# Moving two head pairs of the next batch's scores into the slot of the low-rank down-projection

## Chip, cores and metric

The kernel runs on one core of one Trainium2 chip. The metric is the device time of one launch in microseconds (us). Three runs of the kernel before gave 316.07, 316.18 and 316.94 us, median 316.18 us.

## What is computed

Sliding-window causal attention (window 64) over 8 batches, 8 heads, 576 tokens and head size 64, then a mixer: a low-rank mixing over the tokens, and a two-layer MLP over the 512 channels, each with a residual.

```python
scores = scale * np.matmul(q, k.transpose(0, 1, 3, 2))
mask = (rel >= 0) & (rel < window)          # window = 64
attn = softmax(np.where(mask, scores, -1e9))
x = np.matmul(attn, v)                      # -> (8, 576, 512), heads side by side

h = x.transpose(0, 2, 1) @ U @ V            # over tokens, rank 32
u = x + h.transpose(0, 2, 1)
out = u + np.maximum(u @ w_ch1, 0.0) @ w_ch2   # 512 -> 2048 -> 512
```

## The kernel before

**Two streams in one program.** The MLP works on 4608 tokens as nine chunks `c` of 512 tokens. Each chunk has 32 slots. Slots 0 to 15 are the up-projection: `ch1(i)` issues four matmuls of 128x512 into a PSUM tile `psA` (L671) and a ReLU that writes `c1[i]`, on VectorE for the `i` in `DVE_RELU`/`DVE_RELU_N` and on ScalarE for the others. Slots 16 to 31 are the down-projection: `ch2(t, quarter)` issues four matmuls into `psU` (L694), and each fourth one ends with the residual add on VectorE (`osb`, L703) and a store that SyncE issues (L706). So slots 19, 23, 27 and 31 end with a store.

**The next batch rides along.** While chunk `c` runs, the pieces of batch `b = c + 1` are put behind single slots: a table `PLACE` (with `PLACE_1`, `PLACE_2`, `PLACE_3` for the first batches) gives for each kind of piece the slot after which it is issued. There is no scheduler: each engine's instructions stand in the order in which this loop issues them, and an engine waits at an instruction until its semaphores are there.

```python
for fill, extra in zip(mlp(c) + [lambda: None], slots):
    fill()
    for f in extra:
        f()
```

The kinds of pieces are:

- **T**, from batch 2 on: `TX(t)`, two DMA transposes (L311) that SyncE issues, one for the keys (`kf<-kr`) and one for the queries (`qf<-qr`) of the 128 tokens of tile `t`, t = 0 to 4. They stand in the chunk that `CROSS` names, otherwise in slots 20 to 24 of chunk `b - 3`. They write one of two buffers, by the batch's parity. SyncE's queue also holds the stores of the output and the UT transposes, all in one order.
- **S**: first `SC8` (the last block of queries for all heads, tiles `low` and `high`), then `SC(j)` for the four head pairs j = 0 to 3: 36 matmuls of 64x64 or 64x128 into `sc` for two pairs (L352), and an exponential on ScalarE into `pts[:, j]` (L372). An `SC(j)` reads the transposed tiles t = 0 to 3 of its batch in this order; block pairs that cross into tile 3 need its queries.
- **M**: the 0/1 mask on VectorE, one for `SC8` (L385) and one for each head pair (L378).
- **PV**: `PVA`, the products with the values into four PSUM tiles, then the division on VectorE into `xs` (L470 to L493).
- **U**: `UM`, the low-rank down-projection from `xs` into `pshh` (L513, L521) and a copy to `hh` on ScalarE (L528).
- **V**: `VM`, the up-projection of the rank into `psv` (L593) and the addition on VectorE into `un` (L606), for tiles (0, 1), (2, 3) and (4).
- **UT**: a DMA transpose of `un` into the MLP's operand `uTc` (L621), from batch 3 on; SyncE issues it. Chunk 3 needs tiles 0, 1 and 2 of batch 3.

Before the change the entries for the steady batches were these, so that all five scores of a batch stood in slots 0 and 3 of its own chunk:

```python
"S": [0, 0, 0, 3, 3],
"M": [0, 1, 2, 4, 5],
"PV": [8],
"U": [14],
"V": [16, 17, 18],
"UT": [17, 17, 18, 18, 19],
```

**PSUM.** `ps_big` (two tiles of two banks, tag `big`) serves `sc`, `xw`, `pshh` and `psv` in turn; `ps_tp` (one bank) serves `low`, `one` (the last values of a batch) and the transposes of the first batches; `psum["mm"]` has three banks for `psA`, `psU`, `high` and `xe`.

**Loads.** GpSimd's queue loads K, Q and V of later batches and casts them (L128, L137, L142).

Of the kernel before, what the change touches and what calls it, by code (L numbers as in the profile page):

```python
# [12 lines left out]
FP32 = mybir.dt.float32  # L13
# [3 lines left out]
def kernel(  # L17
# [12 lines left out]
    B, H, S, D = q.shape  # L30
# [3 lines left out]
    P = nc.NUM_PARTITIONS  # L34
# [12 lines left out]
    CH = 512  # L47
# [17 lines left out]
    ps_big = ctx.enter_context(tc.tile_pool(name="ps_big", bufs=2, space=bass.MemoryType.PSUM))  # L65
    ps_tp = ctx.enter_context(tc.tile_pool(name="ps_tp", bufs=1, space=bass.MemoryType.PSUM))
# [81 lines left out]
    def shift_v(b, copy, tiles):  # L148
        va, vb = vA[b % 2], vB[b % 2]
        lo, hi = tiles.start, tiles.stop  # L150
        copy(out=vb[W:P, lo:hi, :, :], in_=va[W:P, lo:hi, :, :])
        last = min(hi, NFULL - 1)
        if lo < last:
            copy(out=vb[0:W, lo:last, :, :], in_=va[0:W, lo + 1 : last + 1, :, :])

    def shift_high(b, copy, t):
        copy(out=vB[b % 2][W:P, t, :, :], in_=vA[b % 2][W:P, t, :, :])  # L157
# [103 lines left out]
    def attention(b, spare=False):  # L261
# [6 lines left out]
        pcs = {}  # L268
# [106 lines left out]
        def MK(j):  # L375
            def f():
                dst = pts[:, j, :, :, :].rearrange("p g n w -> p g (n w)")
                nc.vector.tensor_tensor(  # L378
                    out=dst, in0=dst, in1=maskA.rearrange("p g n w -> p g (n w)"), op=ALU.mult
                )  # L380
            return f
# [25 lines left out]
        def values(dst, h, blk):  # L407
            if blk == 0:
                rhs = va[:, 0, h, :]
            elif blk % 2 == 1:  # L410
                rhs = va[:, blk // 2, h, :]
            else:
                rhs = vb[:, blk // 2 - 1, h, :]
            nc.tensor.matmul(  # L414
                dst,
                pts[:, h // 2, h % 2, blk, :] if blk < NB - 1 else ptl[:, h // 2, h % 2, :],
                rhs,
                start=True,
                stop=True,
            )  # L420

        def PV(t):
            def f():
                blks = [bl for bl in (2 * t - odd, 2 * t + 1 - odd) if 0 <= bl < NB]
                lo = W if (odd and t == 0) else 0
                hi = W if (not odd and t == NT - 1) else P

                xr = ps_big.tile([P, 2, CH], FP32, name="xr", tag="big")
                for h in range(H):
                    for blk in blks:  # L430
                        r0 = ((blk + odd) % 2) * W
                        cols = slice((h % 4) * VW, (h % 4 + 1) * VW)
                        values(xr[r0 : r0 + W, h // 4, cols], h, blk)
                xv = xr[lo:hi, :, 0 : 4 * VW].rearrange("p a (h e) -> p a h e", e=VW)
                rcp = wk_pool.tile([P, 2, 4, 1], FP32, name="rcp", tag="rcp")
                nc.vector.reciprocal(out=rcp[lo:hi], in_=xv[:, :, :, D:VW])
                nc.vector.tensor_tensor(
                    out=x[lo:hi, t, :, :].rearrange("p (a h) d -> p a h d", a=2),
                    in0=xv[:, :, :, 0:D],
                    in1=rcp[lo:hi].to_broadcast([hi - lo, 2, 4, D]),  # L440
                    op=ALU.mult,
                )
            return f
# [56 lines left out]
        hh = {}  # L500
        xc = lambda src, t, dc: src[:, t, :, :].rearrange("p h d -> p (h d)")[:, dc * P : (dc + 1) * P]

        def UM(ts):
            def f():
                if ts[0] == 0:
                    if spare:
                        hh["ps"] = psum["spare"].tile([P, CH], FP32, name="psh", tag="spare")
                    else:
                        hh["ps"] = ps_big.tile([P, 2, CH], FP32, name="pshh", tag="big")[:, 0, :]
                for t in ts:  # L510
                    xt = x[:, t, :, :].rearrange("p h d -> p (h d)")
                    if t < 4:
                        nc.tensor.matmul(  # L513
                            hh["ps"][t * R : (t + 1) * R, :], ub[odd][:, t, :], xt,
                            start=True, stop=False,
                        )
                        continue

                    for g in range(4):
                        cols = slice(g * P, (g + 1) * P)  # L520
                        nc.tensor.matmul(  # L521
                            hh["ps"][g * R : (g + 1) * R, cols], ub[odd][:, t, :], xt[:, cols],
                            start=False, stop=True,
                        )
                if ts[-1] == NT - 1:
                    hh["sb"] = wk_pool.tile([P, CH], BF16, name="hh", tag="hh")
                    for cs in (slice(0, CH // 2), slice(CH // 2, CH)) if spare else (slice(0, CH),):
                        nc.scalar.copy(out=hh["sb"][:, cs], in_=hh["ps"][:, cs])  # L528
            return f
# [108 lines left out]
        if not spare:  # L638
            pcs["M"] = [MK(j) for j in range(HP)]
            pcs["M"].insert(0 if b >= NGR else HP, MK8)  # L640
        pcs["PV"] = [PVA] if not spare else [PV(t) for t in range(NT)]
        pcs["U"] = [UM((t,)) for t in range(NT)] if spare else [UM(tuple(range(NT)))]
        if spare:
# [12 lines left out]
        return pcs  # L656


    DVE_RELU = {0: (7, 9, 11, 15), 1: (4, 7, 9, 10, 11, 13, 14), 2: (2, 3, 4, 6, 7, 8, 10)}
    DVE_RELU_N = (0, 1, 2, 4, 5, 6, 8)  # L660

    def mlp(c):
        uTc = uT_of(c)
# [2 lines left out]
        def ch1(*ids):  # L666
            def f():
# [10 lines left out]
                for i in ids:  # L678
                    c1[i] = c1_pool.tile([P, CH], BF16, name=f"c1_{i}")
                    if i in DVE_RELU.get(c, DVE_RELU_N):  # L680
                        nc.vector.tensor_relu(out=c1[i][:], in_=ps[i][:])  # L681
# [32 lines left out]


    PLACE = {
        "S": [0, 0, 0, 3, 3],
        "M": [0, 1, 2, 4, 5],
        "PV": [8],
        "U": [14],  # L720
        "V": [16, 17, 18],
        "UT": [17, 17, 18, 18, 19],
    }
    PLACE_0 = {"V": [0, 0, 1, 2, 2, 3, 4, 4]}
    PLACE_1 = {
# [21 lines left out]
        "SV": [7, 7, 8, 8],  # L747
        "PV": [10],
        "U": [16],
        "V": [18, 19, 20],  # L750
        "UT": [18, 18, 19, 19, 20],
    }
    CROSS = {
        0: {2: [16, 17, 18, 19, 20]},
# [82 lines left out]
    for c in range(NCH):  # L837
        slots = all_slots[c]

        def place(b, parts, where):  # L840
            if b not in att:
                att[b] = attention(b)
            for part in parts:
                for f, s in zip(att[b][part], where[part]):
                    all_slots[c + s // 100][s % 100].append(f)

        b = c + 1
        if b < B:
            if b == 1:
                for _ in load_kq(2, False):  # L850
                    pass

            def load_next(b=b):
                for _ in load_kq(b + 2, False):
                    pass

            if 1 < b and b + 1 < B:
                load_v(b + 1)
            if 1 < b and b + 2 < B:
                load_next()  # L860
            where = {1: PLACE_1, 2: PLACE_2, 3: PLACE_3}.get(b, PLACE)
            if b < NXB:
                place(b, ("T",), where)
            if b == 1:
                place(0, ("V",), PLACE_0)
                slots[6].append(lambda: nc.scalar.copy(out=ub[1][:], in_=uf[1][:]))
            if 3 < b + 1 < B:
                slots[24].append(
                    lambda bs=b + 1: shift_v(bs, nc.vector.tensor_copy, range(NFULL))
                )  # L870
            if b <= 3:

                def land(t, b=b):
                    def f():
                        shift_high(b, nc.scalar.copy, t)
                        if t > 0:
                            shift_low(b, nc.vector.tensor_copy, t - 1)
                    return f

                att[b]["SV"] = [land(t) for t in range(NFULL)]  # L880
                place(b, ("SV",), where)
            place(b, ("S", "M", "PV"), where)
            for n, at in CROSS.get(c, {c + 3: CROSS_N}).items():
                if n < B:
                    place(n, ("T",), {"T": at})
            place(b, ("U", "V", "UT"), where)
            if b == 1:

                def after(t):
                    return lambda: nc.gpsimd.tensor_copy(  # L890
                        out=held[:], in_=qfs[0][0:1, t * HP * P : t * HP * P + 1]
                    )

                slots[20] += [after(2), lambda: load_v(2), after(NT - 1), load_next]
# [4 lines that stand above are left out]
# [30 lines left out]
```

## Time and profile before

| | before |
|---|---|
| time, median of 3 runs | 316.18 us |
| profiled execution, its own time | 316.14 us |
| its span, first to last instruction | 314.4 us |
| TensorE matmul busy | 306.2 us, 97% of the span |
| VectorE / ScalarE / GpSimd busy | 162.4 / 110.8 / 98.8 us |
| first `psA` matmul of chunk 2 / 3 / 4 | 94.06 / 126.73 / 158.81 us |
| last load issued on GpSimd's queue | 184.0 us |

The profile is one execution. "PE" is TensorE's matmuls, "PEld" its weight loads, DVE VectorE, ACT ScalarE, POOL GpSimd, and SPq the issue of DMAs on SyncE. The chain is the work that ended last, followed back from the end. A timeline row gives start and duration in us, engine, line, operation and tiles (output, then inputs), and a count where rows are merged; in square brackets is the engine's idle time before it, and what ended it. A DMA's row on SPq is the time of its issue; the time to its landing is longer and is told apart.

### The profile page before, as it was taken

Reading aid. Unit: us, or ns where it says so; the run is one execution under the profiler, and the core shown is the slowest. Engines: PE = TensorE matmul, PEld = TensorE weight load, DVE = VectorE, ACT = ScalarE, POOL = GpSimd, SP = SyncE. Lnnn points to the kernel's source line nnn. Section 1 sums busy time; section 2 is a strip of 40 time slices with the busy share of each in tenths; the row PEclk is TensorE's granted clock in tenths of the full one; section 3 lists DMA queues with packets and bytes.
Section 4 is the critical chain, followed back from the end, with each engine's and each line's share of the span. In section 5 each row is a group of like instructions: output and inputs, shape, how many; then the busy total and the mean of one; then the engine's idle time right before and its main releaser. Section 6 shows DMA issues by size and latency. Waiting matters only on the chain.

```text
span 314.4 us, 6910 instructions
## 1 busy us (share of the span) xinstructions
PE 306.2 (97%) x2875; PEld 149.3 (47%) x2875; DVE 162.4 (52%) x297; ACT 110.8 (35%) x178; POOL 98.8 (31%) x129
## 2 busy tenths in 40 slices
PE   8889999999999999999999999999999999999994
PEld 7444554544454544454445444544454444444441
DVE  4465477428645944684358445844574343016011
ACT  3575590358127620633053304440344003201500
POOL 8584154279555445343553440000000000000000
PEclk9999999999999999999999999999999999999999
DMA  7999999999999999999999999924100510011011
GB/s 112 162 187 207 196 163 139 153 196 172 137 151 188 157 166 183 174 143 152 158 174 145 174 152 156 163 68 118 69 2 2 149 68 2 33 67 35 0 67 67
DMA packets 152255, 39.34 MB, mean 125 GB/s; under 512 B 140928, under 2 KB 147072, under 8 KB 152224
## 3 DMA queue, kind: packets, MB, share of 16 engines
q0 software_dynamic: 100624, 18.36, 77.9%
q1 hardware_dynamic: 51600, 20.55, 38.3%
q8 instruction: 22, 0.36, 0.5%
q14 instruction: 9, 0.07, 0.1%
HBM read 36.92 MB, written 9.44 MB: 147 GB/s over the span
## 4 chain that ended last, share of the span: by engine, by line
PE 91%; DMA 4%; DVE 3%; ACT 1%; issue 0%; POOLq 0%
PE psA L671 40%; PE psU L694 36%; PE psv L593 3%; PE sc L352 3%; DMA uTc<-un 2%; PE xw L414 2%; DMA kr<-in_k_dram 2%; PE tpg L288 1%; DVE xs L481 1%; PE sc L342 1%; PE tpu L625 1%; PE pshh L513 1%; ACT pts L372 1%; PE tpm L288 1%; PE xr L414 1%
## 5 line engine op out<-in xcount | busy, mean ns | idle before, releaser
L671 PE MATMUL psA<-uTc,w1b 128*128 128x512 bf16 x576 | 130.8, 379 | 0.7 <-DVE uTc L580 0.4
L694 PE MATMUL psU<-w2b,c 128*128 128x512 bf16 x576 | 131.2, 379 | 0.1
L694 PEld LDWEIGHTS <-c 128*128 128x128 bf16 x576 | 55.5, 98 | 65.7 <-issue 0.8
L671 PEld LDWEIGHTS <-w1b 128*128 128x128 bf16 x576 | 54.1, 98 | 65.3 <-issue 2.7
L683 ACT ACTIVATE c<-psA 128x512 bf16<-128x512 f32 x84 | 50.1, 597 | 89.5 <-PE psA L671 88.5
L703 DVE TENSOR_TENSOR osb<-psU,un 128x512 f32<-128x512 f32 x36 | 24.7, 691 | 75.5 <-PE psU L694 75.2
L681 DVE TENSOR_SCALAR c<-psA 128x512 bf16<-128x512 f32 x60 | 41.4, 690 | 27.5 <-PE psA L671 27.5
L606 DVE TENSOR_TENSOR un<-psv,xs 128x512 bf16<-128x512 f32 (+1 forms) x40 | 25.6, 685 | 22.9 <-PE psv L593 22.7
L128 POOL DMA_DIRECT2D kr<-in_k_dram x30 | 25.4, 848 | 24.2 <-DMA vA<-in_v_dram 14.3
L137 POOL DMA_DIRECT2D vA<-in_v_dram x32 | 28.3, 893 | 15.1 <-DMA kr<-in_k_dram 4.0
L372 ACT ACTIVATE pts<-sc 128x1024 bf16<-128x1024 f32 x32 | 31.3, 1030 | 3.9 <-PE sc L352 3.9
L128 POOL DMA_DIRECT2D qr<-in_q_dram x30 | 25.4, 846 | 21.5 <-DMA vA<-in_v_dram 13.6
L405 ACT ACTIVATE ptl<-low 128x256 bf16<-128x256 f32 x6 | 2.3, 384 | 62.0 <-PE high L352 62.0
L378 DVE TENSOR_TENSOR pts<-pts,maskA 128x1024 bf16<-128x1024 bf16 x28 | 19.1, 682 | 0.1
L481 DVE TENSOR_TENSOR xs<-xw,rcw 128x896 bf16<-128x896 f32 x14 | 15.3, 1092 | 0.5
L352 PEld LDWEIGHTS <-kf 64*64 64x64 bf16 x704 | 9.7, 107 | 7.3 <-issue 7.1
L593 PE MATMUL psv<-hh,vrep 128*128 128x512 bf16 x40 | 12.6, 379 | 0.0
L352 PE MATMUL sc<-qf,kf 64*64 64x128 bf16 (+1 forms) x608 | 11.5, 212 | 0.7 <-DVE qf L305 0.5
L414 PEld LDWEIGHTS <-pts 128*64 128x64 bf16 x512 | 9.9, 110 | 4.3 <-issue 3.0
L628 ACT COPY uTc<-tpu 128x512 bf16<-128x512 bf16 x9 | 5.3, 585 | 10.8 <-PE tpu L625 10.8
L157 ACT COPY vB<-vA 64x520 bf16<-64x520 bf16 x15 | 8.4, 618 | 0.4 <-DMA vA<-in_v_dram 0.3
L414 PE MATMUL xw<-vA,pts 128*64 128x65 bf16 x217 | 8.5, 195 | 0.0
(108 smaller groups left out, 162.8 us busy)
## 6 DMA issues: line engine op xcount, KB each, us to landing
out_dram<-osb SPq DMA_DIRECT2D x36, 256.0 KB, 3.9
vA<-in_v_dram POOLq DMA_DIRECT2D x32, 128.0 KB, 13.4
kr<-in_k_dram POOLq DMA_DIRECT2D x24, 128.0 KB, 11.9
qr<-in_q_dram POOLq DMA_DIRECT2D x24, 128.0 KB, 11.7
w2b<-in_moe_w_ch_dram POOLq DMA_DIRECT2D x4, 512.0 KB, 15.3
w1b<-in_moe_w_ch_dram POOLq DMA_DIRECT2D x2, 512.0 KB, 11.1
w1b<-in_moe_w_ch_dram POOLq DMA_DIRECT2D x1, 1024.0 KB, 9.1
kr<-in_k_dram POOLq DMA_DIRECT2D x2, 288.0 KB, 5.4
```

The costliest lines, as they stand in the source:

```text
L128: nc.gpsimd.dma_start(out=dst[0:rows, t, :, :], in_=src[b, :, t * P : t * P + rows, :].rearrange("h p d -> p h d"),)
L137: nc.gpsimd.dma_start(out=va[:, t, :, 0:D], in_=v[b, :, t * P : (t + 1) * P, :].rearrange("h p d -> p h d"),)
L352: nc.tensor.matmul(sc[g][r0 : r0 + W, col * W : (col + n) * W], keys_of(j, u, rs), queries_of(j, blk, n, rs), start=not spare, stop=last o ...
L372: nc.scalar.activation(out=dst, in_=sc[:], func=ACT.Exp, scale=scale)
L414: nc.tensor.matmul(dst, pts[:, h // 2, h % 2, blk, :] if blk < NB - 1 else ptl[:, h // 2, h % 2, :], rhs, start=True, stop=True,)
L593: nc.tensor.matmul(ps[0][:, n, :], vrep[:, off : off + P], hh["sb"][:], start=True, stop=True)
L606: nc.vector.tensor_tensor(out=u_tiles[g][rs, :], in0=ps[0][rs, n, :], in1=x[rs, t, :, :].rearrange("p h d -> p (h d)"), op=ALU.add,)
L671: nc.tensor.matmul(ps[i][:], w1b[:, dc, i * P : (i + 1) * P], uTc[:, :, dc, :], start=(dc == 0), stop=(dc == NDC - 1),)
L681: nc.vector.tensor_relu(out=c1[i][:], in_=ps[i][:])
L683: nc.scalar.activation(out=c1[i][:], in_=ps[i][:], func=ACT.Relu)
L694: nc.tensor.matmul(acc[t][:], c1[i][:, t * P : (t + 1) * P], w2b[:, i, :], start=(i == 0), stop=(i == NFC - 1),)
L703: nc.vector.tensor_tensor(out=osb[:], in0=acc[t][:], in1=u_tiles[g][:], op=ALU.add)
```

## The change

From batch 4 on (`AHEAD = 4`) the list S of a batch is cut: `SC8`, `SC(0)` and `SC(1)` stay in slot 0 of its own chunk, and `SC(2)` and `SC(3)` become "S+", with their masks as "M+". S+ and M+ of batch `b + 1` are placed while batch `b` is, in the chunk before their own: directly behind `UM` of batch `b`. For the steady batches that is slot 11, and PV, U and their masks move to it: PV from slot 8 to 5, U from 14 to 11, V and UT one slot sooner. In chunk 2, where batch 3 is prepared, U stays in slot 16, S+ of batch 4 goes behind it, and V and UT move one slot later. `pshh` is taken from `ps_tp` rather than from `ps_big`, for all batches but batch 0. The ReLUs that VectorE takes in steady chunks change from 0, 1, 2, 4, 5, 6, 8 to 0, 1, 2, 4, 11, 12, 13. The number of instructions does not change.

```diff
@@ UM @@
-                        hh["ps"] = ps_big.tile([P, 2, CH], FP32, name="pshh", tag="big")[:, 0, :]
+                        hh["ps"] = ps_tp.tile([P, CH], FP32, name="pshh", tag="tp")[:]
@@ attention, the lists of pieces @@
+        if b >= AHEAD:
+            for part in "SM":
+                pcs[part + "+"] = pcs[part][3:]
+                pcs[part] = pcs[part][:3]
@@
+    AHEAD = 4
+
-    DVE_RELU_N = (0, 1, 2, 4, 5, 6, 8)
+    DVE_RELU_N = (0, 1, 2, 4, 11, 12, 13)
@@ PLACE @@
-        "S": [0, 0, 0, 3, 3],
-        "M": [0, 1, 2, 4, 5],
-        "PV": [8],
-        "U": [14],
-        "V": [16, 17, 18],
-        "UT": [17, 17, 18, 18, 19],
+        "S": [0, 0, 0],
+        "M": [0, 1, 2],
+        "PV": [5],
+        "U": [11],
+        "S+": [11, 11],
+        "M+": [13, 14],
+        "V": [15, 16, 17],
+        "UT": [16, 16, 17, 17, 18],
@@ PLACE_3 @@
-        "V": [18, 19, 20],
-        "UT": [18, 18, 19, 19, 20],
+        "S+": [16, 16],
+        "M+": [17, 18],
+        "V": [19, 20, 21],
+        "UT": [19, 19, 20, 20, 21],
@@ the placing loop @@
-            place(b, ("U", "V", "UT"), where)
+            place(b, ("U",), where)
+            if AHEAD <= b + 1 < B:
+                place(b + 1, ("S+", "M+"), where)
+            place(b, ("V", "UT"), where)
```

## Prediction

> **What bounds the kernel now.** I read the page's busy times first, then the chain of work that ended last, then the timelines of TensorE and SyncE where the change acts.
>
> ```profile
> PE 306.2 (97%) x2875; PEld 149.3 (47%) x2875; DVE 162.4 (52%) x297; ACT 110.8 (35%) x178; POOL 98.8 (31%) x129
> PE 91%; DMA 4%; DVE 3%; ACT 1%; issue 0%; POOLq 0%
> ```
>
> TensorE bounds it, and its matmuls hardly wait: the chain runs through PE for 91%. A busy PE need not be at its peak, so I take starts. Where the MLP runs alone the chain has 64 `psA` in 13.81 us, 0.216 us each, 0.863 us a slot. Against that pace two waits are left in the middle of the kernel: 0.22 us at 52.84 us, and 0.38 us where chunk 3 begins, for `uTc`. The rest of the excess is about 0.09 us at each turn between 128x512 matmuls and the smaller ones: `psA` x12 at 128.38 takes until 131.08, 2.70 us for 12 x 0.216 = 2.59. So only turns can be saved, and any new wait on PE is added in full.
>
> TensorE around U of chunk 2 and chunk 3, where S+ will stand (timeline):
>
> ```profile
> 111.92 0.40 PE L513 MATMUL pshh<-xs,ub 128*32 128x512 bf16 x4
> 112.30 1.90 PE L694 MATMUL psU<-w2b,c 128*128 128x512 bf16 x8
> ...
> 126.73 1.02 PE L671 MATMUL psA<-uTc,w1b 128*128 128x512 bf16 x4 [0.22 <-DMA uTc<-un]
> 131.08 0.65 PE L352 MATMUL sc<-qf,kf 64*64 64x128 bf16 x36
> 131.66 1.69 PE L671 MATMUL psA<-uTc,w1b 128*128 128x512 bf16 x7
> ...
> 142.66 0.40 PE L513 MATMUL pshh<-xs,ub 128*32 128x512 bf16 x4
> ```
>
> The two pairs that move cost 131.66 - 131.08 = 0.58 us and a turn. What they read comes from SyncE's transposes. These are the issues for tile 3 of batch 4's keys and queries, and for the first and last that batch 5's moved scores need:
>
> ```profile
> 105.89 2.08 SPq L311 DMA_TRANSPOSE kf<-kr  x1
> 108.08 1.23 SPq L311 DMA_TRANSPOSE qf<-qr  x1
> ...
> 124.23 1.48 SPq L311 DMA_TRANSPOSE kf<-kr  x1
> 136.19 2.35 SPq L311 DMA_TRANSPOSE qf<-qr  x1
> ```
>
> The rows are issues only. The trace's answer on the tile `qf`, cut to the one at 108.08 and then to the one at 136.19, gives from issue to landing:
>
> ```profile
> DMA to landing us min/median/max: 7.9/7.9/7.9
> DMA to landing us min/median/max: 10.1/10.1/10.1
> ```
>
> So batch 4's queries of tile 3 are there at 108.08 + 7.9 = 116.0, batch 5's at 146.3. In the same way batch 6's (issued 163.59, 9.4 us) land at 173.0 and batch 7's (197.95, 4.5 us) at 202.5. Before, each is first read in its own chunk, 10 or more us later.
>
> [...] So a score that waits holds up all `psA` and `psU` behind it. [...] the last matmul starts at 310.5 and the granted clock is 0.50 from 313.8:
>
> ```profile
> 310.50:313.80 3.30, 0.01 (x1) 0.00 (x0) 0.69 (x1) 0.00 (x0) 0.00 (x0) 1.00 0.21 79
> 313.80:314.40 0.60, 0.00 (x0) 0.00 (x0) 0.00 (x0) 0.00 (x0) 0.00 (x0) 0.50 0.00 0
> ```
>
> The third column from the right is the clock. [...] `uTc` transposes land in 2.4 us at best, after the loads are done, but in 7.2 us at 119.39.
>
> **The change, part by part.**
>
> *Turns.* S in slot 3 had two turns and U two; U and S+ in one slot have three. Four batches (4 to 7) save one each: 4 x 0.09 = -0.4 us. Bounds: 0 (turning from U to S+ costs two), -0.75 (it costs none).
>
> *Chunk 2, S+ of batch 4.* U ends at 112.30 (unchanged up to there: PE and SyncE have the same order). S+ starts at 112.4, does the pairs within tiles 0 to 2 (the last landed at 112.7), and stands until 116.0 + 0.1. A third of the 0.58 us is done before, so 0.39 remains: end 116.5 instead of 113.0. **+3.5 us** (3.2 to 3.8). Behind it on PE is every `psU` of chunk 2, on ScalarE two exponentials (1.03 us each), on VectorE two masks, then the `un` additions that feed UT.
>
> *Chunk 3's start.* V is now in slot 19. After a turn and slots 17 to 19 (3 x 0.863) `psU` of that slot ends at 119.2; VectorE's `osb` (0.69) and two additions (0.68 each) end at 120.1, 120.8, 121.4. SyncE's order is now store, UT(0), UT(1), UT(2): 120.1 + 1.2 for the store as at 118.08, 1.3 each, so UT(2) is issued at 124.0 and lands with 7.2 us at 131.2. PE has finished chunk 2 at 116.5 + 15 x 0.863 + 5 x 0.216 + 0.1 = 130.6. It waits 0.6 to 0.7 us where it waited 0.38: **+0.3 us** (-0.4 if landing takes under 6.6 us, +1.2).
>
> *Chunk 3, S+ of batch 5.* SyncE goes on: UT(3), UT(4), the store of slot 23, and batch 5's first transpose at 128.6 instead of 124.23. From that to the landing of the eighth took 146.3 - 124.2 = 22.1 us here, 20.4 for batch 6, 19.5 for batch 3; [...] I take 21.3: landing 149.9 (bounds 148.1, 150.7). Chunk 3 starts at 131.3. U came 15.93 us after the start; without three slots and slot 3's scores it comes 15.93 - 2.59 - 0.68 = 12.66 after: 143.9, S+ at 144.4. It stands until 150.0; less the 0.2 us done before: **+5.4 us** (3.6 to 6.9, with SyncE a little late).
>
> *Chunk 4, S+ of batch 6.* Let S+ of chunk 3 end at E. UT(0) follows 4.8 us later, and as in chunk 3 before (146.14 to 152.60, to a landing at 173.0) batch 6 is in at E + 4.8 + 26.9 = E + 31.7. PE needs 18.6 us to chunk 4 and 13.2 to S+: E + 31.8. A tie: **+0.2 us** (0 to 1.5). Batch 7's transposes took 16.7 us, shorter by 3.7: no wait.
>
> *The clock.* The wait in chunk 2 is 3.2 us idle, just under what the end of the trace shows; that in chunk 3 about 5.4. [...] I take 0.6 x 2 = **+1.1 us** (0 to 2.9; more if chunk 2 is caught too).
>
> *At nothing.* Values three slots sooner: their loads are in (batch 5's last at 147.9, read after 165; batch 4's 117.5, read after 137). `pshh` in `ps_tp`: the tile before it there is `one`, emptied by the last of the divisions (L493), which U awaits anyway; were that cover gone it would cost 0.4 us a batch. Masks and ReLUs: from slot 11 to 19 VectorE has 3 ReLUs, 2 masks and 5 additions, 10 x 0.68 = 6.8 us, in some 9 us of PE (8 slots, U, S+, `psv`); ScalarE has the copy and two exponentials, 2.6 us, before its next ReLU 2.6 us later, and three `psA` banks between.
>
> *Sum:* 3.5 + 0.3 + 5.4 + 0.2 + 1.1 - 0.4 = 10.1. The profiled execution took 316.14 us in all, 0.04 below the median, so **326.2 us**.
>
> **Rivals.**
>
> 1. *Only turns change* (faster or same). If the transposes land before S+ reaches them, 315.4 to 316.2. It is decided at 112.4 and 144.4: tile 3 must have landed. SyncE issues in the same order up to 108.08, so chunk 2's landing can only move by noise. Against it: 3.6 us. Chance 0.03.
> 2. *Only the first wait.* PE's own delay gives SyncE time. It would need batch 5 in 5 us sooner, a landing of 5 us instead of 10, seen only once loads end. 316.2 + 3.5 + 0.3 - 0.4 = 319.6, with a rest up to 321.5. Chance 0.10.
> 3. *Half clock twice, and a wait in chunk 4.* 326.2 + 1.8 + 2 + 1.5 = 331.5 and more. Chance 0.10.
> 4. *VectorE becomes the bound* behind the masks: only if slots 11 to 19 hold over 9 us of its work; they hold 6.8. It would add under 0.5 us a chunk, and is in the range.
>
> **Numbers.** The main case has 0.77: 322 to 330.5. With some of 2 and 3 the range is 321.5 to 331. A measurement here tells about 0.3% (0.95 us) from no change. Faster by that 0.01 (even all turns saved give 0.75), same 0.02, slower 0.97.
>
> **What would show it.** In the profile after: `sc` L352 waiting for DMA `qf` in chunk 2 near 112.5 for 3 us and in chunk 3 near 144.5 for 5, a new share of DMA in the chain, PEclk below 9 in the slice after. No wait in chunk 5. I am wrong if the chain stays on PE throughout, if chunk 3 shows under 3 us, or if the delay sits on DVE or ACT.

## Result and profile after

The changed kernel is slower: 331.40 us median of 4 runs (327.89 to 333.51) beside 316.56 us for the kernel before, also 4 runs; the ratio is 1.043, with a 95% interval of 1.034 to 1.052. This ratio, like all below, leaves out executions more than 1.5% above the fastest of their kernel, here the one of 333.51, which the medians take in. The profiled execution of the changed kernel took 327.89 us, 11.75 us more than that of the kernel before, and its span is 326.2 us.

The page's busy times, clock and chain, as they were read before:

```profile
PE 309.5 (95%) x2875; PEld 150.9 (46%) x2875; DVE 163.5 (50%) x297; ACT 111.4 (34%) x178; POOL 98.9 (30%) x129
PEclk9799999999999999995999999999999999999999
PE 70%; DMA 15%; issue 5%; POOL 4%; DVE 3%; ACT 1%; POOLq 0%
```

No engine got more instructions. The chain has lost 21 points on PE and gained 11 on DMA, and one slice in the middle has half the clock. TensorE's timeline at the moved scores shows where; first chunk 2 (batch 4's pairs), then the start of chunk 3, then batch 5's pairs in chunk 3:

```profile
115.34 0.35 PE L352 MATMUL sc<-qf,kf 64*64 64x128 bf16 x12
116.28 0.50 PE L352 MATMUL sc<-qf,kf 64*64 64x128 bf16 x24 [0.58 <-DMA qf<-qr]
...
131.81 1.02 PE L677 MATMUL psA<-uTc,w1b 128*128 128x512 bf16 x4 [0.89 <-DMA uTc<-un]
...
144.85 0.30 PE L352 MATMUL sc<-qf,kf 64*64 64x128 bf16 x8
146.22 0.25 PE L352 MATMUL sc<-qf,kf 64*64 64x128 bf16 x4 [1.07 <-DMA qf<-qr]
150.85 0.80 PE L352 MATMUL sc<-qf,kf 64*64 64x128 bf16 x24 [4.38 <-DMA qf<-qr]
```

Of the 36 score matmuls 8 or 12 go at once; the other 24, among them those that read the queries of tile 3, stand in the bracket, and every `psA` and `psU` stands behind them. The bracket counts from the modelled end of the matmul before. Taken from start to start against TensorE's pace (0.216 us for 512 columns, 0.58 us for 36 scores), these waits are 0.75, 1.05, 1.23 and 4.57 us.

The time from one chunk's first `psA` to the next shows the sum:

| from the first `psA` to the next chunk's, us | before | after | difference |
|---|---|---|---|
| start of the span to chunk 0 | 23.55 | 25.69 | +2.14 |
| chunk 0 | 37.30 | 38.20 | +0.90 |
| chunk 1 | 33.21 | 33.21 | 0 |
| chunk 2 | 32.67 | 34.71 | +2.04 |
| chunk 3 | 32.08 | 39.67 | +7.59 |
| chunks 4 and 5 | 64.19 | 63.97 | -0.22 |
| chunk 6 | 32.09 | 31.40 | -0.69 |

The first two rows lie ahead of all moved scores; of the edit they hold only the other PSUM tile of batch 1's `pshh`, in chunk 0. In this execution the granted clock was 0.50 from 11.4 to 14.8 us; in the profiled execution of the kernel before it was 1.00 from 6.6 to 26.7. These 3.0 us are not the change: `late` and `no_loads` below have the same `pshh`, start chunk 0 at 23.95 and 23.55, and take 37.30 for it. Chunk 2 holds 0.58 us of scores more than before, which chunk 6 is rid of; the rest of its +2.04 is the first two waits, the second counted against the 0.38 that stood there before. Chunk 3 has 5.8 us of waits and half clock behind them:

```profile
140.00:147.91 7.91, 5.40 (x42) 2.25 (x40) 3.94 (x7) 3.57 (x6) 3.11 (x4) 1.00 1.98 158
147.91:154.73 6.82, 3.88 (x32) 1.80 (x32) 0.69 (x1) 1.94 (x2) 2.12 (x3) 0.50 1.80 151
154.73:160.00 5.27, 5.27 (x26) 2.35 (x24) 4.76 (x8) 1.19 (x2) 4.49 (x6) 1.00 2.46 153
```

A row is a stretch of time, its length, the busy time of PE, PEld, DVE, ACT and POOL with their instructions, then the granted clock, the DMA share and GB/s. TensorE had 3.88 us of work at half clock, so about 1.9 us were lost.

### The profile page after: what moved, and what is told of

Same layout as the page of the kernel before. It is cut to its first block, busy times and chain, and to the rows that moved or that the text cites. A ratio compares the mean times of both kernels' runs of the same rounds, so it can differ in the third digit from the quotient of the medians.

```text
span 326.2 us, 6912 instructions
## 1 busy us (share of the span) xinstructions
PE 309.5 (95%) x2875; PEld 150.9 (46%) x2875; DVE 163.5 (50%) x297; ACT 111.4 (34%) x178; POOL 98.9 (30%) x129
## 4 chain that ended last, share of the span: by engine, by line
PE 70%; DMA 15%; issue 5%; POOL 4%; DVE 3%; ACT 1%; POOLq 0%
PE psA L677 31%; PE psU L700 28%; DMA kr<-in_k_dram 7%; DMA vA<-in_v_dram 3%; DMA qf<-qr 3%; PE sc L352 2%; DMA qr<-in_q_dram 2%; PE psv L593 2%; POOL qr L128 2%; POOL kr L128 1%; PE xw L414 1%; POOL vA L137 1%; DVE xs L481 1%; PE tpg L288 1%; PE tpm L288 1%
## 5 line engine op out<-in xcount | busy, mean ns | idle before, releaser
L677 PEld LDWEIGHTS <-w1b 128*128 128x128 bf16 x576 | 54.8, 98 | 67.3 <-issue 4.6
L352 PE MATMUL sc<-qf,kf 64*64 64x128 bf16 (+1 forms) x608 | 12.6, 215 | 7.5 <-DMA qf<-qr 6.0
L528 ACT CAST hh<-pshh 128x512 bf16<-128x512 f32 x7 | 4.1, 585 | 15.0 <-PE pshh L521 15.0
```

What stands on the lines that cost most here:

```text
L352: nc.tensor.matmul(sc[g][r0 : r0 + W, col * W : (col + n) * W], keys_of(j, u, rs), queries_of(j, blk, n, rs), start=not spare, stop=last o ...
L677: nc.tensor.matmul(ps[i][:], w1b[:, dc, i * P : (i + 1) * P], uTc[:, :, dc, :], start=(dc == 0), stop=(dc == NDC - 1),)
```

## Experiments

Theory A is the prediction's: TensorE waits for the landing of transposes that SyncE issues, at a time that the DMA queues set. Theory B puts the loss on VectorE, ScalarE and PSUM at the new slots. Theory C puts it on the clock. All ratios are to the kernel before on the same chip (medians of 316.13 to 317.51 us), with a 95% interval.

**The same kernel again (`again`).** No edit.

> The changed kernel once more, for a second profile of it. Theory A (TensorE stands at the moved scores until SyncE's transposes have landed, an absolute time set by the DMA queues): the first wait depends on how late TensorE comes, so start-up delay is absorbed in chunk 2 (0 to 3.5 us there), chunk 3 waits 5 to 6 us, half clock for about 7 us after it, 328 to 333 us. Theory B (VectorE and ScalarE are late with masks, ReLUs and exponentials at the new slots): TensorE's waits sit at psA and psv behind DVE or ACT, in every one of chunks 3, 4 and 5.

329.78 us, ratio 1.037 (1.032 to 1.043). The profiled execution, 332.19 us, is one of the longer ones of this kernel, so I use it for the spread alone. TensorE comes to batch 4's pairs earlier, at 113.05, and waits longer; their last transpose was issued at 109.8 and landed 8.5 us later.

```profile
118.34 0.79 PE L352 MATMUL sc<-qf,kf 64*64 64x128 bf16 x24 [4.50 <-DMA qf<-qr]
136.78 1.02 PE L677 MATMUL psA<-uTc,w1b 128*128 128x512 bf16 x4 [2.33 <-DMA uTc<-un]
155.12 0.80 PE L352 MATMUL sc<-qf,kf 64*64 64x128 bf16 x24 [4.87 <-DMA qf<-qr]
```

The waits sit in the same three places. Chunks 4 and 5 take 31.99 us each, so theory B's steady loss is not there, as it was not in the table. Delay from the start-up is taken back in chunk 2, as theory A says: the first profiled execution of the changed kernel begins chunk 2 at 97.10 and chunk 3 at 131.81, that of `no_loads` below 94.06 and 132.21.

**The moved scores read older data (`other_buffer`).**

```diff
+        ko, qo = (f[1 - odd].rearrange("p (t j w) -> p t j w", t=NT, j=HP) for f in (kfs, qfs))
 def keys_of, queries_of:
-            return kx[rs, u // 2, j, ...]
+            return (ko if early[0] else kx)[rs, u // 2, j, ...]      # queries the same, with qo
 def SC(j):
+                early[0] = b >= AHEAD and j >= 2
```

> The changed kernel with the order of every engine kept, but the moved scores of a batch read the transposed keys and queries of the batch before it (the other of the two buffers), which landed some 30 us earlier. Those two head pairs are thus computed from the wrong batch. Theory A: both waits go, and with them the half clock; 315.8 us, at most 0.4 below the kernel before. Theory B: nothing goes, about 331 us, since masks, ReLUs, exponentials and PSUM tiles are where they were. Theory C (the waits were only a small part, the half clock does the rest on its own): above 318 us.

316.96 us, ratio 0.999 (0.997 to 1.001). In chunk 2:

```profile
112.70 0.65 PE L358 MATMUL sc<-qf,kf 64*64 64x128 bf16 x36
113.28 0.82 PE L708 MATMUL psU<-w2b,c 128*128 128x512 bf16 x3
```

All 36 scores run through in 0.58 us. Slots, masks, ReLUs, exponentials and PSUM tiles are those of the changed kernel, and the loss is gone: waiting for the landing of the transposes is its cause, and B falls. The mean granted clock of its profiled execution is 1.0 (0.983 in the changed kernel's), so without the waits for the scores no half clock is seen there, and C falls as the main cause. Chunks 3 to 5 take 31.98 to 31.99 us instead of 32.08 to 32.10: the saved turn, 0.10 us each. The wait for `uTc` at the start of chunk 3 stays, 0.79 us.

**The pairs nine slots later (`late`).**

```diff
 PLACE:    -"S+": [11, 11], "M+": [13, 14]    +"S+": [20, 20], "M+": [21, 22]
 PLACE_3:  -"S+": [16, 16], "M+": [17, 18]    +"S+": [22, 22], "M+": [23, 24]
```

> The changed kernel with the moved pairs still in the chunk before their own, but nine slots later (slot 20, with masks at 21 and 22; for batch 4 slot 22, masks 23 and 24) and so on their own, not with the down-projection. Theory A: TensorE reaches them at about 118.6 and 147.9 in chunks 2 and 3, after their transposes at 116.0 and 146.3, so no wait or under 1 us; a turn more for each batch than in the changed kernel, so no gain either: 316.2 to 317.2 us. If having the scores in the chunk before is bad in itself (PSUM tiles, ScalarE between the psU slots): 320 us or more.

316.97 us, ratio 0.999 (0.997 to 1.002). In chunk 2:

```profile
119.08 0.85 PE L352 MATMUL sc<-qf,kf 64*64 64x128 bf16 x36
```

The scores are still in the chunk before their own; only the slot is late enough. Those of chunk 3 run at 150.06 without a wait.

**Zero matmuls in the place of the waits (`warm`).**

```diff
+    WARM = {3: 15, 4: 26}      # batch being prepared: matmuls of 128x512 from `idle`
+    def keep_busy(n): ...      # into a tile of psum["mm"] that nothing reads
+                if b in WARM:
+                    slots[where["U"][0]].append(lambda n=WARM[b]: keep_busy(n))
                 place(b + 1, ("S+", "M+"), where)
```

> The changed kernel with matmuls of zeros put on TensorE between U and the moved scores, whose result nothing reads: 15 of 128x512 in chunk 2 (3.2 us) and 26 in chunk 3 (5.6 us), about as long as the waits there. Theory A: they take the place of idle time, so the waits go and the scores come when they did, but the clock stays at full speed through both chunks: 2.0 us (half clock after chunk 3 alone) to 3.6 us (after both) below the changed kernel, 326 to 328 us. If the half clock costs nothing here: as the changed kernel, 330 us. If the waits were not for an absolute time: 8.8 us more, 338 us.

326.86 us, ratio 1.032 (1.028 to 1.035). The mean granted clock of its profiled execution is 1.0, and the scores of chunk 2 no longer wait:

```profile
112.40 3.41 PE L670 MATMUL busy<-idle 128*128 128x512 bf16 x15
115.75 0.65 PE L352 MATMUL sc<-qf,kf 64*64 64x128 bf16 x36
```

Those of chunk 3 hardly do: they take 0.8 instead of 0.6 us. The 8.9 us of added matmuls (41 x 0.216) cost nothing beyond the changed kernel; they only fill its waits. The median is 3 to 4.5 us below the two of the changed kernel, but the intervals overlap; the clock's price is better read from the windows above and below.

**No loads behind batch 5's keys and queries (`no_loads`).**

```diff
-            if 1 < b and b + 1 < B:
+            if 1 < b and b + 1 < 5:
                 load_v(b + 1)
 def load_next:
+                if b + 2 > 5:
+                    loaded[b + 2] = (kn[b % 2], qn[b % 2])
+                    return
```

> The changed kernel without the loads after batch 5's keys and queries: values of batches 5 to 7 and keys and queries of 6 and 7 are left out, so these batches work on older data; all instructions of the other engines stay. The DMA engines are free of loads from about 135 us on. If the transposes land late because the loads share the engines with them: batch 5's last one lands some 3 to 5 us after its issue at 139 instead of 8 to 10, at 142 to 144, just when TensorE comes, so the wait of chunk 3 (5 to 6 us) and the half clock behind it nearly go, while that of chunk 2 stays: 321 to 324 us. If SyncE's queue alone sets the landing: as the changed kernel, 328 to 332 us.

322.27 us, ratio 1.019 (1.013 to 1.025). The answers on batch 5's last needed transpose (`qf`, issued at 142.29 in the changed kernel, at 140.26 here) are, from issue to landing:

```profile
DMA to landing us min/median/max: 8.5/8.5/8.5
DMA to landing us min/median/max: 2.5/2.5/2.5
```

Without the loads it is in at 142.8, and TensorE, which comes at 145.25, does not wait. The issue is only 2.0 us earlier, the way from issue to landing 6 us shorter. So SyncE's queue alone does not set the landing; the loads that are under way at the same time lengthen it; by what means the run does not show. The wait of chunk 2, where the loads still run, stays at 3.45 us.

**One batch at a time (`only4`, `only5`).** `AHEAD` becomes a set of batches; chunks whose own scores are whole keep the old table and the old ReLU choice (chunk 2 too where batch 4 is not moved). In `only5` the pairs follow U in slot 14 of chunk 3.

```diff
-        if b >= AHEAD:
+        if b in AHEAD:             # (4,) or (5,)
-            if AHEAD <= b + 1 < B:
+            if b + 1 in AHEAD:
+    PLACE_OLD = the table before, with "S+": [14, 14], "M+": [15, 15]
```

> Only batch 4's two head pairs go ahead, in slot 16 of chunk 2 as in the changed kernel; chunk 3 has the new table, later ones the old table and the old choice of ReLUs. Theory A: the wait of chunk 2 alone, 3.5 to 5 us, with up to 1.6 us of half clock and up to 2 us more at the start of chunk 3, where uTc is late; nothing in chunks 3 to 5: 320 to 325 us. If the wait of chunk 3 comes from chunk 3's own table: as the changed kernel.

324.17 us, ratio 1.023 (1.018 to 1.028).

> Only batch 5's two head pairs go ahead, behind U in slot 14 of chunk 3 (old table and old ReLU choice there), about 2.6 us later in the chunk than in the changed kernel, and with no wait in chunk 2 ahead of it. Theory A: TensorE comes at about 143.2 to 144, the last transpose lands at 146.3 to 148; a wait of 3 to 4 us in chunk 3 alone, [...]: 319 to 322 us. If the wait of chunk 3 was handed on from chunk 2: 316.2 us.

321.48 us, ratio 1.011 (1.006 to 1.016). `only4` waits in chunk 2 and `only5` in chunk 3, each without the other:

```profile
116.03 0.50 PE L352 MATMUL sc<-qf,kf 64*64 64x128 bf16 x24 [3.59 <-DMA qf<-qr]
147.83 0.80 PE L352 MATMUL sc<-qf,kf 64*64 64x128 bf16 x24 [3.40 <-DMA qf<-qr]
```

So the second wait stands without the first. In `only4` the wait is 3.75 us from start to start, and 1.59 us follow at the start of chunk 3 for `uTc`. Its windows before, in and behind the half clock (the third column from the right is the granted clock):

```profile
113.00:117.06 4.06, 1.02 (x27) 0.68 (x27) 0.00 (x0) 0.71 (x1) 1.34 (x3) 1.00 2.08 141
117.06:120.47 3.41, 3.19 (x9) 1.18 (x8) 1.39 (x2) 1.23 (x2) 2.53 (x4) 0.50 1.98 197
120.47:124.00 3.53, 3.53 (x18) 1.57 (x17) 2.98 (x5) 0.00 (x0) 2.79 (x4) 1.00 2.43 156
```

3.41 us at half speed hold 9 matmuls where the next 3.53 us hold 18: about 1.7 us lost. This is the shortest of the four executions of `only4`. Its mean clock is 0.995, that of the other three 0.987 to 0.989: by twice the missing share of the clock times the span I estimate 7 to 8 us at half clock in them instead of 3.4.

**Late batches alone (`ahead7`, `only67`).** The same edit with 7, or with 6 and 7. `ahead7` kept the new ReLU choice in all chunks.

> Only batch 7's two head pairs go ahead (slot 11 of chunk 5, with the new table for batch 6 and 7); batches 4, 5 and 6 keep the old table, pshh and the ReLU choice are the new ones. Theory A: batch 7's transposes land at about 202.5, PE comes to the scores at about 204, so no wait; one turn of TensorE saved, 0.1 us: 316.1 us. Theory B: the steady chunk with the new slots costs what chunk 4 or 5 would, some 2 to 5 us: 318 to 321 us.

318.16 us, ratio 1.003 (0.999 to 1.006). Batch 7's pairs stood in slot 14 here, not 11 as that text has it, since batch 6 kept the old table. They did not wait; chunks 3 to 5 each lost 0.6 us before the last `psA`, which is the ReLU choice and has its own run below. So this run says nothing clean on batch 7.

> Only batches 6 and 7 go ahead: batch 6 behind U in slot 14 of chunk 4 (old table), batch 7 in slot 11 of chunk 5 (new table); the old ReLU choice where the old table is used. Theory A: batch 6's last transpose lands at about 173, TensorE comes at about 175; batch 7's at 202.5, it comes at about 205; no waits, two turns saved, 0.2 us below the kernel before: the same within the measurement. If moving scores ahead is bad wherever it is done: 4 us or more above.

317.21 us, ratio 1.003 (1.0015 to 1.0047). Batch 6 does not wait, batch 7 does, 0.97 us from start to start. I had expected none:

```profile
205.99 0.50 PE L352 MATMUL sc<-qf,kf 64*64 64x128 bf16 x24 [0.81 <-DMA qf<-qr]
```

The transposes landed at 206.0 in this execution and not at 202.5. In the changed kernel this wait is absent: the last transpose needed is issued at 207.85 and lands 4.0 us later, and TensorE comes only at 216.51.

**The ReLU choice alone (`relu_alone`).** The kernel before with `DVE_RELU_N = (0, 1, 2, 4, 11, 12, 13)`.

> The kernel before with the new choice of ReLUs for VectorE (0, 1, 2, 4, 11, 12, 13) alone. In the run with batch 7 alone, three chunks with the old slots and this choice waited 0.6 us each for a psA bank behind the division. Four or five chunks (3 to 6, and 7 and 8 without attention work) then cost 1.8 to 3 us: 318 to 319 us. If the choice is harmless on its own: 316.2 us.

319.68 us, ratio 1.009 (1.006 to 1.011). In each of chunks 3 to 6:

```profile
142.12 1.02 PE L671 MATMUL psA<-uTc,w1b 128*128 128x512 bf16 x4 [0.44 <-DVE c L681]
```

With values still in slot 8, VectorE's ReLUs 11 to 13 stand behind the divisions, and a `psA` bank is late by 0.60 us from start to start. The choice and the earlier slot of the values belong together; neither costs anything in `other_buffer`, which has both.

**A later shared slot (`u18`).** U and S+ at slot 18, V at 20, UT at 21, the old ReLU choice; batch 4's pairs alone at slot 22.

```diff
 PLACE: "PV": [8], "U": [18], "S+": [18, 18], "M+": [20, 21], "V": [20, 21, 22], "UT": [21, 21, 22, 22, 23]
 PLACE_3: "S+": [22, 22], "M+": [23, 24], "V": [18, 19, 20], "UT": [18, 18, 19, 19, 20]
```

> The scores still share a slot with the down-projection in the steady chunks, but at slot 18 rather than 11 (values stay in slot 8, V 20 to 22, UT 21 to 23, old ReLU choice); batch 4's pairs stand alone in slot 22 of chunk 2. TensorE reaches them at about 146 in chunk 3 (transposes landed at 146.3 in the kernel before), 179 in chunk 4 (173), 211 in chunk 5 (202.5). Theory A: no wait over 1 us, one turn saved in chunks 3 to 5, 0.3 us in all: 315.9 to 317 us, the same or a trace faster. If moving U and V is itself harmful (uTc late at the next chunk): 318 us or more.

325.23 us, ratio 1.022 (1.017 to 1.026). The scores of chunk 3 do not wait, but chunk 4 does:

```profile
147.05 0.65 PE L352 MATMUL sc<-qf,kf 64*64 64x128 bf16 x36
166.15 1.86 PE L677 MATMUL psA<-uTc,w1b 128*128 128x512 bf16 x4 [6.03 <-DMA uTc<-un]
```

UT in slots 21 to 23 stands in SyncE's queue between and behind the batch transposes of slots 20 to 22, four of them ahead of the first. I had not counted them. Half clock follows the wait: these four `psA` take 1.79 us to the next start, for 0.95 at the start of chunk 3 in the kernel before, and the mean granted clock is 0.989. Chunk 4 takes 34.07 us. No version here beats the kernel before: the most to be had is the turns, and `other_buffer`, free of every wait for the scores, is 0.1% below it, within its interval.

## Why the prediction was right or wrong

The direction, both places and the releaser were right, and so was the forecast that chunk 5 would not wait and that VectorE's and ScalarE's work lies at nothing. The term that was mis-sized is the clock. Step by step:

- *Turns, -0.4.* Right: 0.10 us a chunk in chunks 3 to 6.
- *Chunk 2, +3.5.* Right without start-up delay: 3.75 (`only4`) and 3.45 (`no_loads`). The profiled execution of the changed kernel came 3 us later and waited 0.75. The landing itself moved more than the noise I had allowed it: 116.3 in that execution, 118.3 in that of `again`.
- *Chunk 3's start, +0.3.* Right where nothing waits ahead of it (0.79 in `other_buffer` against 0.38 before), else too small: 1.05 in the profiled execution and 1.59 in `only4`, so +0.7 to +1.2.
- *Chunk 3, +5.4.* Right: 1.23 + 4.57 = 5.8. Batch 5's last transpose landed at 150.8, for 149.9 predicted.
- *Chunk 4, +0.2.* No wait.
- *The clock, +1.1.* This term was mis-sized. I held chunk 2's 3.2 us of idle time to be just too short, beside the 3.30 us from the last matmul to the half clock at the end of the trace of before, and gave chunk 3's wait a chance of 0.6 and a loss of 2 us; these two were my estimates, which no trace of before showed. Half clock came in chunk 2 as well, with TensorE at work again: in `only4` it resumed at 116.03, and the 4.06 us before half clock began at 117.06 hold 1.02 us of work (first row of its windows). There and in `no_loads`, with 3.3 to 3.6 us idle in chunk 2, 1.7 us were lost (the three slots of `psU` behind the scores took 4.29 us in both, for 12 x 0.216 = 2.59), and behind chunk 3's wait in the changed kernel 1.9. An execution with both loses some 3.6 by this sum. The mean clock of the eight executions of the changed kernel fits: 0.983 or 0.984 in six, 0.979 in the longest (333.51), 0.989 in the shortest (326.52). Twice the missing share of the clock times the span gives an estimate of about 11, 14 and 7 us at half clock, that is three, four and two stretches of the 3.41 us seen in `only4`; in the first profiled execution one of them lies in the start-up.

With the whole wait of chunk 2 and half clock behind both waits the sum of these measured pieces is 3.7 + 1.0 + 5.8 + 3.6 - 0.4 = 13.7 us, 330 us. The two medians of the changed kernel are 331.4, 0.4 us above the range, and 329.8. So the rival of half clock twice, given 0.10, comes closer than my main case, though without its wait in chunk 4. The pieces come from several runs, and six of the eight executions of the changed kernel have no timeline. By the estimate above the longest has 7 us more at half clock than the shortest, at most 3.4 us of the 7.0 us between them; what makes up the rest stays open, and the landing times are one candidate.

*Why moving saves nothing:* a turn is 0.1 us, while the step that is moved reads DMA results that do not come any sooner for it. Rival 2 (only the first wait) failed: batch 5's first transpose, which stands behind chunk 2's stores and UT in SyncE's queue, slipped with TensorE, from 124.23 to the first of these times; the second is the last transpose that the moved scores need, which landed 8.5 us later:

```profile
129.38 1.24 SPq L311 DMA_TRANSPOSE kf<-kr  x1
142.29 1.53 SPq L311 DMA_TRANSPOSE qf<-qr  x1
```

This execution had started 3.0 us late, but in `warm`, which comes to chunk 2 at 94.15, the first transpose is issued at 128.96 all the same.

## What to carry to other kernels

Before a step is pulled forward on the engine that bounds, list when each of its inputs lands and compare with the new time of arrival; slack that the old place had (over 10 us here) is not visible in any wait of the profile. TensorE, whose matmuls start in the program's order in these traces, handed such a wait to everything behind it (in chunk 3 the next `psA` came at 151.59, behind scores that had waited until 150.85), and where the clock fell more was lost, 1.7 to 1.9 us here. A transpose's price here was not its issue (1.53 us) but its landing, which depended on the loads that were under way (8.5 us with them, 2.5 us in `no_loads`).

## Unexpected of the hardware

- TensorE's clock did not fall at one fixed point of a wait. In `only4` TensorE resumed at 116.03 and half clock (granted 0.50) began 1.03 us later; in the changed kernel it began at 147.91, inside a wait that ended at 150.85. The idle stretch in `no_loads` was only 3.3 us, and the clock fell: its mean is 0.994, and the `psU` behind took 4.29 us instead of 2.59. Half clock lasted 3.41 us in `only4` and at the start-up of the changed kernel (11.37 to 14.78), and twice that, 6.82 us, in its chunk 3 (147.91 to 154.73). Two beginnings in `again`, 118.08 and 152.22, are 34.14 us apart, and those two in the changed kernel 136.54 us, about ten and forty times the 3.41 us; the traces do not show why.
- The same DMA transpose, batch 5's last for the queries of tile 3, took 8.5 us from issue to landing beside the loads (changed kernel) and 2.5 us without them (`no_loads`).
